# A long-convolution and expert-routing kernel: fifteen key differences for sixteen keys, the first transform in row halves, the last channel quarter in two halves, and a new order

## The chip, the cores and the metric

The kernel runs on one core of one Trainium2 chip. The core has five engines with queues of their own, each working strictly in its list's order: PE (TensorE, matrix products, with its weight loads shown as PEld), DVE (VectorE), ACT (ScalarE), POOL (GpSimd) and SP, which here issues transfers. [...] The metric is the device time of one execution in microseconds, the median of several runs.

## The reference

The input is 2048 positions by 512 channels, in single precision. Two layers follow one another, each with a residual.

The first normalizes each position, and convolves each channel along the 2048 positions with a kernel of its own, `K[d, l] = 2 Re sum_n C[d, n] exp(A[d, n] dt[d] l)` over 128 modes, plus a skip term. The reference uses FFTs of length 4096.

The second normalizes again and routes to experts:

```python
q = jnp.einsum("nd,dhc->nhc", xf, w_q)            # 32 heads, 2 x 128
s1 = jnp.einsum("nhd,ed->nhe", q[..., :dk], k1)   # 16 keys
s2 = jnp.einsum("nhd,ed->nhe", q[..., dk:], k2)   # 16 keys
i1, i2 = argmax of s1, argmax of s2               # K = 1
top_e = i1 * 16 + i2                              # one of 256 experts
act = gelu(einsum(xf, u[top_e]))
out = einsum(softmax of one score = 1, act, v[top_e])
```

So the scores serve only to find the largest of sixteen in each of 64 groups a position (32 heads, two halves); their size is not used.

## The kernel before, in words

**Constants ahead.** The product of `w_q` and the keys doesn't depend on the position. `w_piece(n)`, 32 pieces, loads a piece of `w_q` (tile wq), multiplies it with the keys (L822), turns it (L830), and stores groups of four pieces to DRAM (w_d, L837). Later the whole is loaded back as w_q, 512 by 1024, and split into a high and a low part (w_hi, w_lo, L917 and L918), so that a product of three fast terms replaces one of full precision.

**Convolution.** It is done by hand-made transforms, in four quarters c = 0 to 3 of 128 channels. For 32 table blocks of 16 channels, POOL builds phase tables (pg, L551) and magnitude tables (mg, L582 and L588), ACT takes sines and cosines (L638 to L641), DVE multiplies them (L645 to L658), and PE sums over the modes (kps, L684): this gives the convolution kernel. pg and mg have two buffers each, so POOL may not fill mg for block i before PE has used block i - 2. Input (u) and kernel (k) then go through the same two transforms. Stage 1 (`stage1`, L465, tiles s1u and s1k) takes eight groups a call in two half-jobs of four groups; ACT copies each from PSUM (L468). Stage 2 (L482, tiles s2yu and s2yk) takes 32 frequencies in eight jobs of four. DVE multiplies the spectra (L726 to L729); in the last quarter POOL does a part (L737), after a copy by ACT (L733). The first inverse transform (ia, L758) has eight jobs a quarter and needs all eight products; its copies (T, L766, in the last quarter L771) go to DRAM (t_d) for c = 0 to 2, and stay on chip for c = 3. All of this shares seven PSUM banks (psA).

**Hand-over and expert part.** When the tables are used up, their memory becomes that of w_q, w_hi and w_lo. Eight blocks b of 256 positions follow: second inverse transform (ib, L1029, from Tb, xt and cb loads), mean and variance, scores (sc, L1143: per 128 positions 4 x 3 x 2 matmuls of 512 columns), products with the experts' first matrix (xu, L1150), then on DVE the maximum of each group (mx, L1165), a comparison with it (eq, L1169), and a product with powers of two (kq, L1174), which POOL adds up within the group (ks, L1180) so that DVE reads the index from the exponent (L1187 to L1191). One-hot masks (oh, L1269), their counts on PE (cnt, L1279), and the product with the experts' second matrix (o, L1313 and L1316) end a block.

**Order.** Each step is entered in a plan with engine, cost, reads and writes, and gets a number. The tuple `ORDER` lists the numbers; the steps are issued in that order, so it fixes each engine's queue, SP's transfers too. The costs are planning numbers and change nothing in the program by themselves.

Of the kernel before, what the change touches and what calls it, by code (L numbers as in the profile page):

```python
# [27 lines left out]
def view(t, off, dims):  # L28
# [135 lines left out]
def kernel(ctx, tc, xa, xb, xt, lar, aim, cre, cim, ldt, dsk, wq, ka, kb, ue, ve,  # L164
# [10 lines left out]
    G.memset(halfpi, math.pi / 2)  # L175
    G.memset(epst, EPS)
    make_identity(nc, ident)

    t_d = dram.tile([P, 3, 2, 2048], F32, name="t_d")
    e_d = dram.tile([P, 11, 256], F32, name="e_d")  # L180
    w_d = dram.tile([P, 4, 1024], F32, name="w_d")

    I = {}

    ab = ctx.enter_context(ExitStack())
    wk = ab.enter_context(tc.tile_pool(name="wk", bufs=1, side="left"))
    ka_s = wk.tile([P, 32], F32, name="ka_s")
# [1248 lines left out]
```

## Time and profile before

| | |
|---|---|
| median of 3 runs | 515.38 us (513.67 to 515.58) |
| the profiled execution | 516.5 us, span 514.7 us |
| mean clock of TensorE in it | 0.977 of full |
| PE busy | 459.3 us, 89% |
| DVE busy | 411.3 us, 80% |
| POOL busy | 321.7 us, 63% |
| ACT busy | 300.4 us, 58% |
| transfers | 61.32 MB, 119 GB/s on average |

Busy time is a share of the whole span, and the kernel has stages with different limits, so each stage is read by itself. A row of the profile reads: line of the kernel, engine, operation, output tile and input tiles, partitions by elements; "x" gives the number of instructions. Matmuls overlap, so the mean duration of one is longer than its distance to the next. In the chain of waits, each piece is what the next one waited for; "issue" there is time for which the profile shows no releaser. A product in single precision issues two load and two matmul instructions.

### The profile page before, as it was taken

The numbers are of one execution on the slowest core, as the hardware profiler recorded it, in microseconds if no ns is written. First come the engines' busy times: TensorE is split into PE (matmuls) and PEld (weight loads), VectorE is DVE, ScalarE is ACT, GpSimd is POOL, SyncE is SP. The second block draws the span as 40 slices with busy tenths as digits, with TensorE's granted clock in tenths as the row PEclk, the third lists the DMA queues.
The fourth block names the chain that finished last, engine by engine and source line by source line (L and its number), as shares of the span: only waits on it lengthen the run. The fifth ranks groups of instructions, "written<-read, shape, count | busy, mean of one in ns | idle before, by whom it ended". The sixth has DMA issues, their size and how long they took to land.

```text
span 514.7 us, 16728 instructions
## 1 busy us (share of the span) xinstructions
PE 459.3 (89%) x7206; PEld 392.3 (76%) x7206; DVE 411.3 (80%) x724; ACT 300.4 (58%) x596; POOL 321.7 (63%) x342
## 2 busy tenths in 40 slices
PE   0275889999999999999998949999999999999995
PEld 0143669888998999899997947877878888786784
DVE  5999898899959988999727573888969596979983
ACT  4867799967897598858964442334152341426240
POOL 4989979999999999996807011760351506263330
PEclk9998699999999999999999998999999999999998
DMA  7969474224043102611056984400162141010012
GB/s 255 385 206 383 127 276 146 65 84 175 3 177 96 40 3 82 202 50 44 1 208 183 292 266 155 144 1 1 54 186 91 30 137 42 1 43 0 2 42 85
DMA packets 27362, 61.32 MB, mean 119 GB/s; under 512 B 2932, under 2 KB 14456, under 8 KB 26136
## 3 DMA queue, kind: packets, MB, share of 16 engines
q1 hardware_dynamic: 27136, 60.11, 34.8%
q8 instruction: 57, 0.93, 0.8%
q10 hardware_dynamic: 152, 0.13, 0.1%
q14 instruction: 17, 0.14, 0.1%
HBM read 46.21 MB, written 14.02 MB: 117 GB/s over the span
## 4 chain that ended last, share of the span: by engine, by line
PE 62%; DVE 15%; ACT 11%; DMA 5%; issue 4%; POOL 2%; SPq 0%; DVEq 0%; ACTq 0%; POOLq 0%
PE sc L1143 18%; PE ia L758 8%; PE s2yk L482 4%; PE kps L684 4%; PE s1k L465 3%; PE xu L1150 3%; PE s2yu L482 3%; PE o L1316 3%; PE cnt L1279 3%; PE s1u L465 2%; PE ib L1029 2%; DMA wq<-wq 2%; ACT t L641 2%; PE bc L1247 1%; ACT t L639 1%
## 5 line engine op out<-in xcount | busy, mean ns | idle before, releaser
L551 POOL TENSOR_TENSOR pg<-PS 128x1024 int32<-128x1024 int32 x32 | 68.9, 2152 | 0.5
L582 POOL TENSOR_TENSOR mg<-TS 128x1024 f32<-128x1024 f32 x32 | 62.6, 1958 | 7.8 <-PE kps L684 4.1
L1180 POOL TENSOR_TENSOR ks<-kq 128x512 f32<-128x512 bf16 x16 | 18.9, 1182 | 56.6 <-DVE kq L1174 53.4
L1269 DVE TENSOR_SCALAR oh<-idxb,ec_s 128x2048 bf16<-128x2048 bf16 (+1 forms) x72 | 46.3, 708 | 8.9 <-ACT idxb L1251 7.0
L758 PE MATMUL ia<-ca_s,U 128*128 128x128 f32 x256 | 49.6, 276 | 0.0
L1053 POOL TENSOR_TENSOR vs<-hc 128x256 f32<-128x256 f32 x8 | 6.5, 815 | 62.5 <-ACT hc L1076 62.5
L1143 PE MATMUL sc<-w_hi,hhi 128*128 128x512 f32 x128 | 45.1, 434 | 0.0
L639 ACT ACTIVATE t<-t,halfpi 128x512 f32<-128x512 f32 x64 | 42.4, 662 | 2.1
L1143 PE MATMUL sc<-w_lo,hhi 128*128 128x512 f32 x128 | 40.8, 400 | 0.0
L638 ACT ACTIVATE t<-pg 128x512 f32<-128x512 int32 x64 | 38.9, 608 | 3.0 <-DVE gf L646 2.0
L1143 PE MATMUL sc<-w_hi,hlo 128*128 128x512 f32 x128 | 40.6, 399 | 0.0
L641 ACT ACTIVATE t<-pg 128x512 f32<-128x512 int32 x64 | 38.2, 608 | 3.2 <-POOL pg L551 2.1
L758 PEld LDWEIGHTS ia<-ca_s,U 128*128 128x128 f32 x256 | 38.9, 192 | 0.0
L758 PE MATMUL ia<-ca_s,yk 128*128 128x128 f32 x192 | 38.2, 281 | 0.4 <-DVE mg L658 0.4
L588 POOL TENSOR_TENSOR mg<-TS 128x512 f32<-128x512 f32 x32 | 37.4, 1171 | 0.4
L684 PE MATMUL kps<-mg 128*32 128x64 f32 x1024 | 34.0, 231 | 3.3 <-DVE mg L658 1.6
L465 PE MATMUL s1u<-c_s,xs 128*64 128x128 f32 x512 | 33.4, 277 | 2.5 <-DVE xs L502 1.6
L482 PE MATMUL s2yk<-yk,c_s 128*128 128x128 f32 x256 | 35.0, 283 | 0.5 <-DVE U L729 0.4
L684 PE MATMUL kps<-gf 128*32 128x64 f32 x1024 | 33.5, 228 | 0.9 <-issue 0.9
L482 PEld LDWEIGHTS s2yk<-yk,c_s 128*128 128x128 f32 x256 | 30.8, 192 | 3.7 <-issue 1.4
L465 PE MATMUL s1k<-c_s,k 128*64 128x128 f32 x512 | 32.8, 284 | 0.3 <-ACT yk L468 0.3
L482 PE MATMUL s2yu<-yu,c_s 128*128 128x128 f32 x256 | 32.6, 279 | 0.3
(197 smaller groups left out, 1380.9 us busy)
## 6 DMA issues: line engine op xcount, KB each, us to landing
wq<-wq SPq DMA_DIRECT2D x25, 512.0 KB, 4.1
t_d<-T SPq DMA_DIRECT2D x24, 256.0 KB, 4.2
Tb<-t_d SPq DMA_DIRECT2D x8, 768.0 KB, 6.0
x<-xa SPq DMA_DIRECT2D x8, 512.0 KB, 6.0
xs<-xb SPq DMA_DIRECT2D x16, 256.0 KB, 4.8
xt<-xt SPq DMA_DIRECT2D x8, 512.0 KB, 3.9
out<-ob SPq DMA_DIRECT2D x7, 512.0 KB, 3.0
c_s<-wq SPq DMA_DIRECT2D x4, 512.0 KB, 8.4
```

The costliest lines, as they stand in the source:

```text
L465: T.matmul(ps[64 * k:64 * k + 64, g, :], lhs8(4 * n + g), c1_s[:, k], start=True, stop=True)
L482: T.matmul(ps[:, k, :], c2_s[:, kk, :], y[:, :, kk, :], start=True, stop=True)
L551: G.tensor_tensor(view(pg, 0, [[32, 2 * NC], [8, 4], [1, 8]]), view(t["PS"], 1024 + off, [[1, 2 * NC], [128, 4], [0, 8]]), view(t["PS"], 8 ...
L582: G.tensor_tensor(view(mg, 0, [[96, NC], [8, 8], [1, 8]]), view(ts, 512 + 8 * o, [[8, NC], [1, 8], [0, 8]]), view(ts, 8 * o, [[8, NC], [0, ...
L588: G.tensor_tensor(view(mg, 64, [[96, NC], [8, 4], [1, 8]]), view(ts, 1536 + o, [[1, NC], [64, 4], [0, 8]]), view(ts, 1024 + 8 * o, [[8, NC ...
L638: A.activation(p, pg[:, :, k], AF.Abs)
L639: A.activation(p, p, AF.Sin, scale=-SINSCALE, bias=halfpi)
L641: A.activation(p, pg[:, :, k], AF.Sin, scale=SINSCALE)
L684: T.matmul(kps[32 * q:32 * q + 32, 2 * g + h, :], m[:, d, 64:96], m[:, d, 0:64], start=(e == 0), stop=(e == 1))
L758: T.matmul(ps[:, g, :], t[:, 4 * n + g].rearrange("p a b -> p (a b)"), ca_s[:, s, :], start=(s == 0), stop=(s == 1))
L1143: T.matmul(ps[:, 512 * h:512 * h + 512], t[x_][:, q, ts], I[w_][:, q, 512 * h:512 * h + 512], start=(q == 0 and x_ == w_), stop=(q == 3 an ...
L1269: V.tensor_scalar(oh[:, :, 0:ln], t["idxb"][:, :, sl], S["ec"][:, 4 * e + j:4 * e + j + 1], None, op0=ALU.is_equal)
```

## The change

**Differences.** After the loads, fifteen keys of each half have the sixteenth subtracted (`differ`). The scores are then fifteen differences a group, 960 columns for 1024, 480 a PSUM bank. The largest is raised to zero by a small operation on DVE (128 by 64, 16 times); where no difference equals it, the sixteenth key is meant: no power is added, and the index formula is bounded to give it. POOL adds two overlapping halves of eight, with the power of the shared one halved. w_d, w_q, w_hi, w_lo, the key tiles and the copies `out2` get narrower accordingly (not shown).

**Stage 1.** Its constant mixed four interleaved channels over all 128 rows, with zeros between the rows of different channels. Now it has two channels a 64-row half; each matmul takes 64 rows and 64 columns, the halves write to two PSUM banks, and both banks are copied after both half-jobs.

**Last quarter.** `SEGS` = 2 for c = 3: stage 2 of the kernel takes half of the channels (16 of 32 groups, 64 columns) and eight frequencies a job, still eight jobs. The first four jobs need only the first two stage-1 calls, and the first four jobs of ia only the first four products.

**Order.** All numbers from 6 on move by one (`differ` is 6), and the list is another one. Read by its steps: before, the last six pieces of w_q's product stand on PE behind the last table block, among the stage-2 jobs of the last quarter; now all 32 stand ahead of the end of the third quarter's ia, with the last store of w_d ahead of that quarter's t_d stores. Before, all eight stage-1 half-jobs of the last quarter's kernel stand behind block 30; now six stand ahead of blocks 30 and 31, and two of the stage-2 jobs as well. At the start, twelve loads of wq stood ahead of the last block of x, now sixteen; eight first products of pieces stood ahead of the first block's kps, now eleven; the exponentials for the second half of the channels moved behind the arctangent on ACT. The planning costs of some steps are changed.

```diff
+        def differ():
+            for t, o in ((ka_s, 0), (kb_s, 16)):
+                V.tensor_scalar(t[:, o:o + 15], t[:, o:o + 15], t[:, o + 15:o + 16], None, op0=ALU.subtract)
...
     def stage1(dst, lhs8, kt, nm, r, tiles, key):
+        job, k = {}, None
         for n in range(2):
-            job = {}
             def mm(n=n, job=job):
-                ps = bank(job, f"{nm}_{n}")
-                for g in range(4):
+                if n == 0:
+                    for h in range(2):
+                        bank(job, f"{nm}_{h}", h)
+                for g in range(4 * n, 4 * n + 4):
                     for k in range(2):
-                        T.matmul(ps[64 * k:64 * k + 64, g, :], lhs8(4 * n + g), c1_s[:, k], start=True, stop=True)
-            def ev(n=n, job=job):
-                A.copy(dst()[:, 8 * kt + 4 * n:8 * kt + 4 * n + 4].rearrange("p g k d -> p g (k d)"), job["ps"])
-            k = plan.add("PE", 0.99, mm, r=r, t=tiles, take="psA", n_mm=16)
-            plan.add("ACT", 0.48, ev, w=[key + (kt, n)], t=tiles, give="psA", after=[k])
+                        for h in range(2):
+                            hs = slice(64 * h, 64 * h + 64)
+                            T.matmul(flat(job[h], 64)[64 * k:64 * k + 64, g], lhs8(g)[hs], c1_s[hs, k], start=True, stop=True)
+            k = plan.add("PE", 0.56, mm, r=r, t=tiles, take=() if n else ("psA", "psA"), after=[k] if n else [], n_mm=32)
+        for h in range(2):
+            def ev(h=h, job=job):
+                A.copy(dst()[:, 8 * kt:8 * kt + 8, :, 2 * h:2 * h + 2],
+                       flat(job[h], 64).rearrange("p g (k d) -> p g k d", d=2))
+            plan.add("ACT", 0.52, ev, w=[key + (kt, h)], t=tiles, give="psA", after=[k])
...
+            sg, nk = k4 * ns // 8, 4 * ns
+            g_, k_ = slice(32 * sg // ns, 32 * (sg + 1) // ns), slice(nk * (k4 % (8 // ns)), nk * (k4 % (8 // ns)) + nk)
+            kts = range(4 * sg // ns, 4 * (sg + 1) // ns)
+            deps = [("yk", c, kt, n) for kt in kts for n in range(2)]
+            def mm(job=job, g_=g_, k_=k_, k4=k4, nk=nk):
+                ps = flat(bank(job, f"s2yk{c}_{k4}"), 512 // nk)
+                for kk in range(k_.start, k_.stop):
+                    T.matmul(ps[:, kk - k_.start, :], c2_s[:, kk, :], spectrum(c, "yk")[:, g_, kk, :], start=True, stop=True)
...
-        deps = [("P", c, k4) for k4 in range(8)]
         for n in range(8):
+            job, sg = {}, n * SEGS[c] // 8
+            deps = [("P", c, k4) for k4 in range(8 * sg // SEGS[c], 8 * (sg + 1) // SEGS[c])]
...
-                    T.matmul(ps[:, 512 * h:512 * h + 512], t[x_][:, q, ts], I[w_][:, q, 512 * h:512 * h + 512],
+                    T.matmul(ps[:, 512 * h:512 * h + 480], t[x_][:, q, ts], I[w_][:, q, 480 * h:480 * h + 480],
...
+            eq, ps = d["eq"].rearrange("p (b g) e -> p b g e", b=2), groups()
+            V.tensor_scalar_max(d["mx"], d["mx"], 0.0)
+            V.tensor_tensor(eq, ps, d["mx"].rearrange("p (b g) -> p b g", b=2).unsqueeze(3).to_broadcast([P, 2, 32, 15]),
+                            op=ALU.is_equal)
...
-            G.tensor_tensor(kt_, d["kq"][:, :, 0:8], d["kq"][:, :, 8:16], op=ALU.add)
+            G.tensor_tensor(kt_, d["kq"][:, :, 0:8], d["kq"][:, :, 7:15], op=ALU.add)
...
-            V.tensor_scalar_add(ef.rearrange("p h a -> p (h a)"), ei, -134.0)
+            V.tensor_scalar(ef.rearrange("p h a -> p (h a)"), ei, -134.0, -7.0, op0=ALU.add, op1=ALU.max)
...
-    c1 = np.zeros((4, 32, 2, 32, 4))
+    c1 = np.zeros((4, 32, 2, 32, 2))
     for q in range(4):
-        c1[q, :, 0, :, q] = np.cos(a)
+        c1[q, :, 0, :, q % 2] = np.cos(a)
...
-    keys = np.tile(np.concatenate([2.0 ** (15 - e)] * 2)[None], (128, 1))
+    key = 2.0 ** (15 - e[:15])
+    key[7] /= 2
+    keys = np.tile(np.concatenate([key] * 2)[None], (128, 1))
```

More of the change, by code (lines that the diff above doesn't have):

```diff
@@ L180 @@
     e_d = dram.tile([P, 11, 256], F32, name="e_d")
-    w_d = dram.tile([P, 4, 1024], F32, name="w_d")
+    w_d = dram.tile([P, 4, 960], F32, name="w_d")
     I = {}
@@ L729, in prod, with part, rest @@
                     V.tensor_mul(uv[0:64], pv[64:128], uv[0:64])
-            def part(job=job, k4=k4):
-                job["ki"] = wk.tile([P, 128, 4], F32, tag="kt", name=f"ki{k4}", bufs=3)
-                A.copy(job["ki"][0:64], job["ps"].rearrange("p k m -> p m k")[64:128])
-            def rest(job=job, k4=k4):
-                uv = four(c, Q[c]["U"], k4).rearrange("p g d k -> p (g d) k")
+            def part(job=job, k4=k4, nk=nk):
+                job["ki"] = wk.tile([P, 512 // nk, nk], F32, tag="kt", name=f"ki{k4}", bufs=3)
+                A.copy(job["ki"][0:64], flat(job["ps"], 512 // nk).rearrange("p k m -> p m k")[64:128])
+            def rest(job=job, views=views):
+                pv, uv, kv = views()
                 G.tensor_tensor(uv[0:64], job["ki"][0:64], uv[0:64], op=ALU.mult)
+            k = plan.add("PE", 0.98 if ns == 1 else 1.15, mm, r=deps + u_k + ["c2"], t=tiles, take="psA", n_mm=8 * ns)
             if c < 3:
-                plan.add("DVE", 2.14, prod, r=[("U", c, k4)], w=[("P", c, k4)], t=tiles, give="psA", after=[k])
+                plan.add("DVE", 2.14, prod, r=u_k, w=[("P", c, k4)], t=tiles, give="psA", after=[k])
             else:
@@ L744, in k_s2 @@
                 a = plan.add("ACT", 0.52, part, w=[ki], t=[ki], after=[k])
-                v = plan.add("DVE", 1.43, prod, r=[("U", c, k4)], t=tiles, give="psA", after=[k, a])
+                v = plan.add("DVE", 1.43, prod, r=u_k, t=tiles, give="psA", after=[k, a])
                 plan.add("POOL", 1.5, rest, r=[ki], w=[("P", c, k4)], t=[ki, f"U{c}"], after=[v])
@@ L776, in k_ia @@
             else:
-                a = plan.add("ACT", 0.70, lambda turn=turn: turn(A.copy, 0), w=[("T", c, n, 0)], t=[f"T{c}"], after=[k])
-                plan.add("DVE", 0.70, lambda turn=turn: turn(V.tensor_copy, 1), w=[("T", c, n, 1)], t=[f"T{c}"], give="psA",
+                a = plan.add("ACT", 0.75, lambda turn=turn: turn(A.copy, 0), w=[("T", c, n, 0)], t=[f"T{c}"], after=[k])
+                plan.add("DVE", 0.75, lambda turn=turn: turn(V.tensor_copy, 1), w=[("T", c, n, 1)], t=[f"T{c}"], give="psA",
                          after=[k, a])
@@ L912, in load @@
         def load(q=q):
-            I[q] = I["pre"].tile([P, 4, 256], F32, tag="xt" if q > 1 else "wq", name=f"w_q{q}").rearrange("p a b -> p (a b)")
+            I[q] = I["pre"].tile([P, 4, 256], F32, tag="xt" if q > 1 else "wq", name=f"w_q{q}").rearrange("p a b -> p (a b)")[:, 0:960]
             nc.sync.dma_start(I[q], w_d[:, q])
         plan.add("SP", 1.7, load, r=["pre"] + [("w_d", h) for h in range(8)], t=[w_t], w=[("w_q", q)], lag=2.6)
-        plan.add("ACT", 0.95, lambda q=q: A.copy(I["hi"][:, q], I[q]), r=[("w_q", q)], w=[("w_hi", q)], t=[w_t])
-        plan.add("DVE", 1.15, lambda q=q: V.tensor_sub(I["lo"][:, q], I[q], I["hi"][:, q]), r=[("w_q", q), ("w_hi", q)],
+        plan.add("ACT", 0.90, lambda q=q: A.copy(I["hi"][:, q], I[q]), r=[("w_q", q)], w=[("w_hi", q)], t=[w_t])
+        plan.add("DVE", 1.08, lambda q=q: V.tensor_sub(I["lo"][:, q], I[q], I["hi"][:, q]), r=[("w_q", q), ("w_hi", q)],
                  w=[("w_lo", q)], t=[w_t], lock=True)
@@ L1155, in scores @@
         for q in range(4):
-            last = plan.add("PE", 1.48, lambda q=q: mm(q), t=tiles, after=[] if last is None else [last],
+            last = plan.add("PE", 1.40, lambda q=q: mm(q), t=tiles, after=[] if last is None else [last],
                             r=[(x, k) for x in tiles] + [("w_hi", q), ("w_lo", q)], take="psC" if q == 0 else None, n_mm=6)
@@ L1195, in gelu @@
             A.activation(act[:, k], jx["ps"], AF.Gelu_apprx_tanh, scale=t["rstd"][:, k:k + 1])
-        a = plan.add("DVE", 1.15, top, w=[m], t=[m], after=[last])
-        plan.add("DVE", 1.15, same, r=[m], w=[e], t=[m, e], give="psC", after=[a])
-        plan.add("DVE", 0.62, weigh, r=[e, "cst"], w=[kq_], t=[e, kq_], lock=True)
+        a = plan.add("DVE", 1.08, top, w=[m], t=[m], after=[last])
+        plan.add("DVE", 1.17, same, r=[m], w=[e], t=[m, e], give="psC", after=[a])
+        plan.add("DVE", 0.58, weigh, r=[e, "cst"], w=[kq_], t=[e, kq_], lock=True)
         plan.add("POOL", 2.8, gather, r=[kq_], w=[s_], t=[kq_, s_])
@@ L1299, in select @@
             if ln == 256:
-                plan.add("ACT", 0.52, high, r=[("wt", p)], w=[("whi", p)], t=[kA, kH])
+                plan.add("ACT", 0.64, high, r=[("wt", p)], w=[("whi", p)], t=[kA, kH])
                 plan.add("DVE", 0.62, low, r=[("wt", p), ("whi", p)], w=[("wlo", p)], t=[kA, kH, kL], lock=True)
```

60 lines of the change are left out of this document (32 added, 28 removed), and 162 rows, old and new, of the table ORDER.

## The prediction

> **What bounds the kernel now.** I read the page first (shares, slices), then busy time by stages, the waits of GpSimd, the chain of waits, and single instructions in order of time.
>
> ```profile
> span 514.7 us, 16728 instructions
> PE 459.3 (89%) x7206; PEld 392.3 (76%) x7206; DVE 411.3 (80%) x724; ACT 300.4 (58%) x596; POOL 321.7 (63%) x342
> PE   0275889999999999999998949999999999999995
> POOL 4989979999999999996807011760351506263330
> GB/s 255 385 206 383 127 276 146 65 84 175 3 177 96 40 3 82 202 50 44 1 208 183 292 266 155 144 1 1 54 186 91 30 137 42 1 43 0 2 42 85
> ```
>
> TensorE (PE) is full from slice 7 on, but for a hole near 300 us; GpSimd (POOL) is full from slice 2 to 18. Three stages, convolution, hand-over and expert part (columns: span, then busy us of PE, PEld, DVE, ACT, POOL):
>
> ```profile
> 57.00:256.00 199.00, 192.93 (x3621) 177.00 (x3611) 174.93 (x298) 165.39 (x315) 186.75 (x168) 0.99 0.29 97
> 256.00:310.20 54.20, 43.75 (x828) 39.85 (x826) 30.14 (x53) 26.68 (x57) 12.50 (x11) 0.97 0.71 228
> 310.20:514.70 204.50, 197.90 (x2286) 159.10 (x2286) 157.62 (x238) 69.55 (x116) 76.40 (x106) 0.98 0.20 63
> ```
>
> The convolution has two limits side by side: PE (192.9 of 199) and POOL (186.8). POOL's tables are a fixed amount of work, and they end here:
>
> ```profile
> 254.72 1.17 POOL L588 TENSOR_TENSOR mg<-TS 128x512 f32<-128x512 f32 x1
> ```
>
> at 255.9, with these waits before (us, times, longest):
>
> ```profile
> POOL mg L582 <- PE kps L684: 4.1, 2, 2.8
> POOL mg L582 <- DVE xs L502: 2.4, 1, 2.4
> POOL PS L542 <- DVE A L336: 1.9, 1, 1.9
> ```
>
> So whatever PE saves, the tables end at most 8.4 us earlier; 4.1 of it waits for PE. The hand-over, from the chain of waits:
>
> ```profile
> 257.55 3.64 PE s1k L465 x64
> ...
> 274.63 4.00 DMA wq<-wq
> ...
> 285.34 7.31 DMA w_q<-w_d
> ...
> 298.62 1.43 PE ib L1029 x85
> ...
> 304.77 4.99 issue
> 310.19 5.98 PE sc L1143 x18
> ```
>
> When the tables end, PE still owes all eight stage-1 half-jobs of the last quarter's kernel (x64 is four of them, 0.91 us each), then the last weight pieces go through DRAM in series (their load, their store, and w_q), and PE waits 5.0 us for the second block, where nothing but loads is open. From table end to first score: 310.2 - 255.9 = 54.3 us. The expert part is PE's (197.9 of 204.5).
>
> **The change, part by part.** *Stage 1.* A half-job was 8 products, 16 instructions of 128 columns, two column halves side by side; it becomes 32 instructions of 64 columns in four quadrants. The nearest row has 64 columns in four column tiles:
>
> ```profile
> 214.58 0.89 PE kps L684 x64
> ```
>
> 32 such take 0.45, with a start seam (126.71 to 127.74, 1.03 against 0.91, is 0.12) up to 0.57; I take 0.47, since the two half-jobs now mostly follow each other. No row shows two row halves at once: the other end is 0.91, or worse (rivals). At 64 half-jobs PE saves 64 x 0.44 = 28 us.
>
> [...]
>
> The copies out write runs of two floats; the copy with runs of four costs the same as the contiguous one, so I add nothing; double price would be 64 x 0.59 = 38 us on an ACT with 34 free, and it would bind.
>
> ```profile
> L468 ACT COPY yk<-s1k 128x512 f32<-128x512 f32 x32 | 18.0, 595 | 2.0 <-PE s1k L465 1.7
> L766 ACT COPY T<-ia 128x512 f32<-128x512 f32 x24 | 13.7, 590 | 3.7 <-PE ia L758 3.7
> ```
>
> One wait is new: a half-job pair takes two of the seven PSUM banks at its start, and ACT's copies follow only after the second half. Should PE, with its next list entries queued behind, stand still 0.47 us for it at each of 32 pairs, that is 15 us, more than the 13 that stay over below; I take 0, because ACT is free 34 us in this stage, and the other end goes into C.
>
> *Order.* In the new list six of the eight half-jobs and the last six weight pieces stand ahead of the tables' end. That is 6 x 0.91 = 5.5 us, and six pieces at twice 11.7 / 25 (this row is one of two like groups, 25 pieces each), 5.6:
>
> ```profile
> L822 PE MATMUL wps<-wq,ka_s 128*32 128x128 f32 x200 | 11.7, 309 | 19.3 <-DMA wq<-wq 17.0 <-issue 2.0 <-DVE mg L658 0.2
> ```
>
> With 4.1 us of earlier tables PE must find 15 us before the end and has 28, so POOL sets it: 255.9 - 4.1 = **251.8**. This holds until a half-job costs 0.91 - 15/64 = 0.68. The bounds are 247.5 (all three waits gone) and later than 255.9 (a rival).
>
> *Last quarter in two halves.* Stage 2 there has twice the matmuls, 64 columns instead of 128, and the full 128-column weights each time:
>
> ```profile
> 174.11 0.89 PE s2yk L482 x8
> ```
> ```profile
> L255 PEld LDWEIGHTS va<-dv,eq x4: 188/191/192, 63.5 to 63.8; 128*128 128x128 f32 x4
> L255 PE MATMUL va<-dv,eq x4: 275/276/324, 63.5 to 63.9; 128*128 128x64 f32 x4
> ```
>
> Four loads whose first and last starts are 0.3 us apart: 0.10 each (the view rounds to tenths) under 64-column matmuls, as under 128 columns (0.89 / 8 = 0.11). So the weights set the pace and a job goes from 0.89 to 16 x 0.11 = **1.76**; the other end is 0.89, half the columns at full gain. I take 1.76, its rows being the same shape. Products and transform:
>
> ```profile
> 268.36 0.69 DVE L726 TENSOR_TENSOR yu<-s2yk,U 128x512 f32<-128x512 f32 x1 [5.28 <-ACT ki L733]
> 269.09 0.68 DVE L727 TENSOR_TENSOR U<-s2yk,U 64x512 f32<-64x512 f32 x1
> ```
> ```profile
> 258.50 0.69 DVE L658 TENSOR_TENSOR mg<-mg,t 128x512 f32<-128x512 f32 x1 [0.63 <-ACT t L639]
> ```
> ```profile
> 280.36 0.39 PE L758 MATMUL ia<-ca_s,yu 128*128 128x128 f32 x2
> ```
> ```profile
> 294.49 0.28 PE L758 MATMUL ia<-ca_s,U 128*128 128x128 f32 x1
> ```
> ```profile
> 282.41 0.74 ACT L771 COPY T<-ia 64x256 f32<-64x256 f32 x2 [1.41 <-PE ia L758]
> 283.18 0.86 DVE L771 COPY T<-ia 64x256 f32<-64x256 f32 x2 [3.32 <-ACT T L771]
> ```
>
> Now the new hand-over, in us after the tables' end, along PE's new list: last table product on DVE 3.3 (259.2 - 255.9); last kernel generation 1.0, at 4.3; two stage-2 jobs and two half-jobs, 2 x 1.76 + 2 x 0.47, at 8.8; ACT's two copies 1.1 (0.59 each, overlapping), at 9.9; four stage-2 jobs, at 16.9. The first half's products (four at 1.45 from 3.3, then POOL's 1.3) are ready at 10.4, and the second's at 16.2 or soon after PE's last job, while the first four transforms run: hidden, and what is gained by the halves. Eight transforms, 14.2 (280.4 to 294.6), at 31.1; last copies 1.6, at 32.7; inverse and mean to the first score 298.6 to 310.2 without the 5.0 wait, 6.6, at **39.3**. Gain 54.3 - 39.3 = 15.0. The weights' way through DRAM (274.6 to 292.7) drops out, since their pieces are stored before and w_q can load once the last tables are used, some 30 us ahead of its use. With stage 2 at 0.89 the sum is 34.1, gain 20.2.
>
> *Fifteen differences.* 384 matmuls go from 512 to 480 columns.
>
> ```profile
> 329.40 1.40 PE sc L1143 x6
> ```
> ```profile
> 401.63 1.44 PE o L1316 x12
> ```
>
> Those are 233 ns for 512 columns and 120 ns for 256, so 0.443 ns a column: 32 x 0.443 x 384 = **5.4 us**. On DVE two large operations (and a smaller one) lose a sixteenth and one small one is added, 16 times each:
>
> ```profile
> L1165 DVE TENSOR_REDUCE mx<-sc 128x64 f32<-128x1024 f32 x16 | 19.5, 1220 | 5.7 <-PE sc L1143 5.6
> L1189 DVE TENSOR_SCALAR ef<-ei 128x64 f32<-128x64 int32 x16 | 6.6, 414 | 0.6
> ```
>
> The maximum and the comparison, of one size, give 2 x 19.5/16 = 2.4 back, the new one takes at most 6.6 (as the last row, of its size): net under +4.2 us on an engine busy 157.6 of 204.5, under PE's cover; 0, or +4.2 where that cover fails. POOL's key sums keep their size (76.4 of 204.5 busy), and the casts and copies of the narrower weights shrink in the hand-over's shadow: 0. The subtraction from the keys, once, on two small tiles, lies beside the first loads: 0 to 0.4.
>
> Sum: -4.1 - 15.0 - 5.4 = -24.5. The profiled execution took 516.5 (span 514.7 and 1.8 around it): 492.0. The median shown, 515.38, is 1.1 below that execution: **491**.
>
> **The rivals.** *A. Weights are loaded faster than their rows say* under the shorter stage 2: gain 29.7, **486**. For it: weight loads overlap in kps (64 in 0.89, from column tiles). Against: L255.
>
> *B. The start and the loads take part of it back.* Sixteen instead of twelve wq loads stand ahead of the last block of x, eleven instead of eight weight pieces ahead of the first kernel generation. 512 KB at 385 GB/s is 1.36 us, four make 5.4 on POOL, whose first reuse of a table waits for that generation (the large decay exponentials, moved behind the arctangent on ACT, push the same way); and if the loads of the second block are still the last to land, the 5.0 stay: -14.1, **501**. For it: slices 1 and 3 at 385 GB/s. Against: POOL has other tables to build meanwhile.
>
> *C. Row halves do not overlap*, or a floor under the starts or the banks hold them: a half-job stays near 0.91. PE's busy time of the first two stages, 236.7, plus 7.0 for the last quarter, plus 2.8 of idle behind the last transform, puts the first score between 303.5 and 309.6 (without and with the 6.1 idle before 256); 306.5 gives -3.7 - 5.4, **506**. For it: no row shows overlap.
>
> *D. Slower: the issue order breaks the column pairs too.* A channel group issues first column half with both row halves, then the second. If row halves exclude each other, only the middle two of four can pair: three turns of 2 x 0.056 instead of two of 0.111, 1.33 a half-job, +0.42 x 64 = 27 us where PE already binds: 506 + 27, **533**. It decides from 1.05 us a half-job (64 x 0.14 = 9.1 eats C's gain).
>
> **How the numbers follow.** Forecast 0.43, A 0.22, B 0.15, C 0.12, D 0.08. The range holds the first three: low end A with POOL's other 4.3 us of waits gone too, 481, and 2 us more for what new lists may save in the expert part's 6.6 idle us, 479; high end just behind B, 504. C and D, 0.20, are left out. A measurement here tells about 0.5% (2.6 us) from no change. Faster: forecast, A, B and two thirds of C, 0.88; same 0.04 (the rest of C); slower 0.08.
>
> **What would show it.** Right: stage-1 groups of 16 matmuls in some 0.23 us where they follow each other; POOL's last table at 250 to 254 without waits for kps; no wq or w_q transfer in the chain behind it; stage 2 of the last quarter near 1.76 a job; first score near 291; score groups of six at 1.32 us, the expert part near 199 us. Wrong: half-jobs above 0.68, which hand the end of the tables back to PE; stage-1 copies well above 0.6; a POOL gap before 60 us; DVE waits turning up ahead of scores.

## The result: 538.1 us, slower by 4.6%

The changed kernel took 538.09 us (median of four, 537.56 to 539.94); the kernel before took 515.18 beside it. The ratio is 1.046, with a 95% interval of 1.042 to 1.049. The forecast was 491. Medians here are over all runs of a kernel; ratios leave disturbed runs of both kernels out, so a ratio can differ a little from the quotient of two medians, and of the later runs the profiles of e10 (512.4 us), e14 (529.4, where its ratio rests on 521.0 and 522.6) and e15 (512.4) are of disturbed ones.

The page of the changed kernel, the span and two rows of busy time and granted clock:

```profile
span 536.2 us, 18906 instructions
PE 454.2 (85%) x8294; PEld 392.6 (73%) x8294; DVE 424.3 (79%) x742; ACT 306.9 (57%) x600; POOL 327.9 (61%) x342
PEclk9999868999998798999999599899999999999999
```

PE's busy time fell by only 5 us, and its clock reads below 9 in eight slices where it did in four. The same stages as in the prediction (columns: span, then busy us of PE, PEld, DVE, ACT and POOL, granted clock, DMA share, GB/s):

```profile
57.00:278.60 221.60, 193.39 (x4723) 173.71 (x4726) 179.54 (x307) 172.86 (x331) 191.43 (x170) 0.93 0.32 105
278.60:330.30 51.70, 47.19 (x852) 45.92 (x846) 30.84 (x54) 23.74 (x45) 10.13 (x9) 0.87 0.54 176
330.30:536.20 205.90, 191.07 (x2292) 158.71 (x2286) 168.26 (x255) 72.81 (x120) 84.78 (x109) 0.99 0.20 65
```

GpSimd's last table ends at 278.6 instead of 255.9, the hand-over takes 51.7 instead of 54.3, the expert part 205.9 instead of 204.5. So all of the loss stands ahead of the end of the tables, where PE is now idle for 28.2 us of the 221.6 behind 57 us (before: 6.1 of 199). The rows of single instructions that set these bounds:

```profile
42.16 0.44 PE L696 MATMUL kps<-mg 128*32 128x64 f32 x8
277.44 1.17 POOL L600 TENSOR_TENSOR mg<-TS 128x512 f32<-128x512 f32 x1
330.34 0.70 PE L1169 MATMUL sc<-w_hi,hhi 128*128 128x480 f32 x2
```

The first kernel generation comes at 42.2 (before: 36.9). The groups of stage 1 (busy us, mean ns | idle just before), first of before, then of after:

```profile
L465 PE MATMUL s1u<-c_s,xs 128*64 128x128 f32 x512 | 33.4, 277 | 2.5 <-DVE xs L502 1.6 <-ACT yu L468 0.9
L465 PE MATMUL s1k<-c_s,k 128*64 128x128 f32 x512 | 32.8, 284 | 0.3 <-ACT yk L468 0.3
```
```profile
L475 PE MATMUL s1u<-c_s,xs 64*64 64x64 f32 x1024 | 24.1, 234 | 7.9 <-issue 3.2 <-DVE xs L514 1.5 <-DVE mg L666 1.5
L475 PE MATMUL s1k<-c_s,k 64*64 64x64 f32 x1024 | 22.2, 236 | 5.3 <-issue 3.7 <-ACT yu L480 0.8 <-DVE gf L661 0.6
L480 ACT COPY yu<-s1u 128x512 f32<-128x512 f32 x32 | 19.0, 642 | 14.9 <-PE s1u L475 14.9
```

The row halves do overlap: 66.2 us of stage 1 became 46.3. But 2.8 us of waits before it became 13.2, half of it called issue, which is time in which PE waited for nothing that the profile shows. Two such waits, as they stand in time, and the waits of the whole run that matter here (us, times, longest):

```profile
162.35 3.03 PE L475 MATMUL s1k<-c_s,k 64*64 64x64 f32 x105 [2.29 <-issue]
177.65 0.59 PE L475 MATMUL s1u<-c_s,xs 64*64 64x64 f32 x11 [3.21 <-issue]
```
```profile
POOL mg L594 <- PE kps L696: 20.6, 9, 6.9
PE s1k L475 <- issue: 3.7, 3, 2.3
PE s1u L475 <- issue: 3.2, 1, 3.2
```

GpSimd now waits 20.6 us for kernel generations on PE (before: 4.1). Its own work up to the end of the tables is the same 233 us in both kernels, so what it waits is what the end of the tables inherits.

### The profile page after: what moved, and what is told of

It is laid out like the page before. It is cut to its first block, busy times and chain, and to the rows that moved or that the text cites. A ratio compares the mean times of both kernels' runs of the same rounds, so it can differ in the third digit from the quotient of the medians.

```text
span 536.2 us, 18906 instructions
## 1 busy us (share of the span) xinstructions
PE 454.2 (85%) x8294; PEld 392.6 (73%) x8294; DVE 424.3 (79%) x742; ACT 306.9 (57%) x600; POOL 327.9 (61%) x342
## 5 line engine op out<-in xcount | busy, mean ns | idle before, releaser
L594 POOL TENSOR_TENSOR mg<-TS 128x1024 f32<-128x1024 f32 x32 | 62.6, 1957 | 27.0 <-PE kps L696 20.6
L737 PE MATMUL s2yk<-yk,c_s 128*128 128x128 f32 (+1 forms) x320 | 46.9, 304 | 2.7 <-ACT yk L480 1.4
L1301 DVE TENSOR_SCALAR oh<-idxb,ec_s 128x2048 bf16<-128x2048 bf16 (+1 forms) x72 | 48.7, 737 | 0.0
L737 PEld LDWEIGHTS s2yk<-yk,c_s 128*128 128x128 f32 x320 | 43.1, 215 | 4.7 <-ACT yk L480 1.7
L1169 PE MATMUL sc<-w_hi,hhi 128*128 128x480 f32 x128 | 42.4, 413 | 0.0
L783 PEld LDWEIGHTS ia<-ca_s,U 128*128 128x128 f32 x256 | 41.0, 202 | 1.1 <-DVE U L753 1.1
L1169 PE MATMUL sc<-w_hi,hlo 128*128 128x480 f32 x128 | 38.9, 385 | 0.0
L1169 PE MATMUL sc<-w_lo,hhi 128*128 128x480 f32 x128 | 38.8, 384 | 0.0
L847 PE MATMUL wps<-wq,ka_s 128*32 128x128 f32 x200 | 12.2, 321 | 25.8 <-DMA pb<-wq 16.9
L696 PEld LDWEIGHTS kps<-mg 128*32 128x32 f32 x1024 | 26.0, 118 | 9.7 <-issue 5.4
L783 PEld LDWEIGHTS ia<-ca_s,yk 128*128 128x128 f32 x192 | 30.1, 197 | 3.7 <-ACT t L650 1.4
```

The source lines that it names most:

```text
L594: G.tensor_tensor(view(mg, 0, [[96, NC], [8, 8], [1, 8]]), view(ts, 512 + 8 * o, [[8, NC], [1, 8], [0, 8]]), view(ts, 8 * o, [[8, NC], [0, ...
L696: T.matmul(kps[32 * q:32 * q + 32, 2 * g + h, :], m[:, d, 64:96], m[:, d, 0:64], start=(e == 0), stop=(e == 1))
L737: T.matmul(ps[:, kk - k_.start, :], c2_s[:, kk, :], spectrum(c, "yk")[:, g_, kk, :], start=True, stop=True)
L783: T.matmul(ps[:, g, :], t[:, 4 * n + g].rearrange("p a b -> p (a b)"), ca_s[:, s, :], start=(s == 0), stop=(s == 1))
L1169: T.matmul(ps[:, 512 * h:512 * h + 480], t[x_][:, q, ts], I[w_][:, q, 480 * h:480 * h + 480], start=(q == 0 and x_ == w_), stop=(q == 3 an ...
L1301: V.tensor_scalar(oh[:, :, 0:ln], t["idxb"][:, :, sl], S["ec"][:, 4 * e + j:4 * e + j + 1], None, op0=ALU.is_equal)
```

## The experiments

Three theories at first: O, the new order is the cost; H, the row halves and the falling clock; I, PE waits for its instructions.

**1. The parts alone.** All three code changes with the old order; the differences alone; the row halves alone; the new order with stage 1 whole.

```diff
 e1  ORDER of before (numbers shifted), code of after
 e2  before, +differ() behind the key load, 960 instead of 1024 score columns, ORDER of before
 e3  before, +stage1() of after, ORDER of before
 e4  after, stage1() of before, ORDER of after
 e1, e3: a pair's first copy moves behind its second half
```

> All three code changes (row halves in stage 1, last quarter in two halves, fifteen differences) with the issue order of the kernel before; a stage-1 copy that came too early for both halves is moved behind the second half, nothing else moves. The changed kernel took 538.1 us, the one before 515.2. Theory O (the new order is what costs the time: first kernel generation at 42 instead of 37 us, weight loads ahead of it, last table end at 278.6 instead of 255.9): with the old order the code's savings show and the old waits remain, 500 to 510, last table end near 255. Theory H (the row halves themselves cost it: while they run the granted clock falls, 0.93 instead of 0.99 between 57 us and the last table end): 525 to 540, granted clock below 0.95 between 60 and 255 us. Theory I (PE waits for its own instructions, 16.6 thousand instead of 14.4 thousand): 515 to 530 with the clock near 0.99 and idle time called issue before the stage-1 lines of over 10 us.

> The fifteen differences alone, on the kernel before with its order; the one subtraction from the keys is put behind their load. All theories of the slowdown leave this part out of the convolution, so 509 to 513: score groups of six at 1.31 us instead of 1.40 take 5 to 6 us off PE in the expert part. If the longer chain on VectorE (maximum, the clamp, comparison) binds instead, the expert part stays at 204 to 206 us and the time at 514 to 517.

> The row halves of stage 1 alone, on the kernel before with its order (the copies of a pair behind its second half). Theory O: PE saves up to 20 us of stage 1, the last table end stays at 255 or comes up to 4 us earlier, 505 to 513. Theory H: granted clock below 0.95 between 60 and 255 us, last table end at 262 or later, 522 to 535. Theory I: clock near 0.99 there, last table end at 255 to 262, idle time called issue before stage 1 of over 10 us, 515 to 522.

> The changed kernel with its own new order, but stage 1 in whole columns as before (512 fewer matmuls; last quarter's halves and the differences stay). Theory O: PE has 20 us more of stage 1 to do in the same order, so 538 or slower, up to 555. Theory H: the clock is back at 0.98 or more between 60 us and the last table end, which comes at 250 to 262; 500 to 515. Theory I: 515 to 530.

Measured: e1 535.7 us (ratio 1.049, 1.038 to 1.060), e2 512.4 (1.001, 0.996 to 1.006), e3 538.7 (1.055, 1.046 to 1.064), e4 522.4 (1.022, 1.013 to 1.031). With the old order the row halves alone cost as much as the whole change, so O falls as the main cause; but e4 shows that the new order, together with the last quarter's halves, costs something too, 10 us against e2. e4 lies in I's range alone; e1 and e3 lie where H had them or above. Neither H nor I is settled by these four. In e2 the expert part shrank as forecast (below), but the first kernel generation came at 40.2 instead of 36.9 and the last table at 258.2 instead of 255.9; at the start VectorE stood waiting for the keys:

```profile
10.00 0.23 DVE L289 TENSOR_SCALAR ka_s<-ka_s 128x15 f32<-128x15 f32 x1 [2.69 <-DMA ka_s<-ka]
40.19 0.44 PE L697 MATMUL kps<-mg 128*32 128x64 f32 x8 [0.98 <-POOL TS L588]
```

In e3 PE's waits before stage 1 have a pattern that no data explains (us, times, longest):

```profile
PE s1u L474 <- DVE gf L657: 4.9, 4, 2.0
PE s1k L474 <- DVE mg L669: 2.9, 3, 1.5
PE s1k L474 <- DVE mg L665: 2.9, 2, 1.7
```

Stage 1 reads nothing of `gf` or `mg`. What these table products free is the PSUM bank of the sine or cosine that they read: `trig` takes its bank from the same seven as stage 1. So theory B was added: the two banks that a pair holds.

**2. Banks.** Whole columns in the row halves' bank structure; fewer users of banks; shorter holding.

```diff
 e5  e3, but  T.matmul(job[h][64*k:64*k+64, x], lhs8(g), c1_s[:, k])   # 128 rows, 128 columns, two banks per pair
 e6  e3, nine entries of ORDER moved, and in trig(), cos only:
-        p = flat(bank(...), 32)
+        p = pg[:, :, k].bitcast(F32)      # in place over the phases, no bank
 e7  e3, first half of each pair moved right ahead of its second in ORDER
 e8  before, with the edit of e6
```

> The kernel before with stage 1 in whole columns, but in the bank structure of the row halves: a pair of half-jobs writes two of the seven PSUM banks from its first half on, and both copies come after its second half; issue order of the row-halves run (538.7 us). The temporaries of the sines and cosines take banks of the same seven. Theory B (the banks are the cost: the pair holds two of them for longer, so PE and ScalarE wait for a free one): as slow as the row halves or slower, since PE has 20 us more to do, 535 to 560. Theory W (the row halves' own instructions are the cost: twice the count, small, a falling clock): 513 to 520.

> The row halves alone (538.7 us, old order), but the 64 cosines are written in place over the phases in SBUF and take no bank; the sines still take one each. Theory B: waits for banks shrink from 25 us on PE to a few, last table end near 255 or earlier, 500 to 520. Theory W: 530 to 540.

> The row halves alone, old order, but the first half of each pair is moved right ahead of its second half, so that the two banks are held for about 1.1 us of PE and two copies. Theory B: a pair holds its two banks for some 5 bank-us instead of 10; waits for banks on PE fall to under 10 us, 508 to 525. Theory W: 530 to 540.

> Control: the kernel before with the cosines in place over the phases and nothing else changed. Theory B: before, PE waits 1.7 us and ScalarE 2.7 us for banks, so little is to be had: 511 to 516. If reading the cosines from SBUF is dearer for VectorE: its table products are then longer than 0.69 us and the time is up to 525.

Measured: e5 531.2 us (1.034, 1.024 to 1.044), e6 567.8 (1.107, 1.098 to 1.117), e7 534.7 (1.039, 1.029 to 1.049), e8 560.1 (1.091, 1.083 to 1.099). e5 runs the very matmuls of before and loses 17 us, between the ranges of B and W: under the old order the bank structure alone is a cost. e7 contradicts B's price: held for shorter, the banks give back 4 us, not 14 to 31. e6 and e8 settle nothing about banks, since the control (e8) was hit by something else: with its second operand in SBUF a table product took 1.2 to 1.5 us on average instead of 0.68, and GpSimd's tables, running beside it, went from 1.17 to 1.44 us (mean ns after the comma):

```profile
L661 DVE TENSOR_TENSOR mg<-mg,pg 128x512 f32<-128x512 f32 x32 | 48.6, 1518 | 0.0
L594 POOL TENSOR_TENSOR mg<-TS 128x512 f32<-128x512 f32 x32 | 46.0, 1440 | 0.4
```

**3. Clock or count.** Each stage-1 product twice, so that PE is not idle. Beside it, three steps towards a better kernel: the subtraction later, the weight pieces early, and the last quarter in halves.

```diff
 e9   e3, and
+                            for _ in range(2):
                                 T.matmul(flat(job[h], 64)[...], lhs8(g)[hs], c1_s[hs, k], start=True, stop=True)
 e10  e2, differ() some 4 us later on VectorE
 e11  e10, weight pieces 20 to 31 where the new ORDER has them
 e12  e11, SEGS = (1, 1, 1, 2)
```

> The row halves alone with the old order (538.7 us, granted clock 0.93 between 57 and 279 us) with every stage-1 product issued twice into the same place: the result is the same, PE has about 25 us more to do, and a half-job costs about what whole columns cost. Known beside it: whole columns in the same bank structure take 531.2 with the clock at 1.00. Theory C (what the row halves lose beyond the banks, 7.5 us, comes from PE standing idle so much that its clock is lowered): with more work the clock stays above 0.97 there and the time is 527 to 538, no longer than with half the work. Theory N (the number of small instructions is the cost): 550 to 565, with idle time called issue ahead of stage 1. Theory P (PE's work sets the pace in this form): 545 to 560 without it.

> The fifteen differences alone with the order of before (512.4 us, of which the expert part 198.6 against 204.6, but the first kernel generation at 40.2 instead of 36.9 us, since VectorE stood 2.7 us before the subtraction for the load of the keys). Now the subtraction stands behind the cosine and sign preparation of the second part, some 4 us later on VectorE, when the keys have landed. If that wait is what took back half of the gain: first kernel generation at 36.9 to 37.6, last table end at 255 to 257, 506 to 510. If the start isn't handed on to the tables' end: 510 to 513.

> As the run with the late subtraction (fifteen differences, old order), but the weight pieces of the last three groups stand where the new order has them, ahead of the last tables; stage 1 whole, last quarter in one half. The hand-over from last table end to first score was 54.2 us before and 46.5 in the run with the new order and whole stage 1. If the weights' way through DRAM was what the hand-over waited for: 44 to 50 us from last table end to first score; PE has 5 to 6 us more before the last table end, which moves by 0 to 6: 500 to 509. If it was not: hand-over stays at 52 to 54 and the time is 507 to 514.

> As the run with the early weights, and the last quarter's stage 2 and transform in two halves as in the change. Its rows price a stage-2 job at 1.9 us instead of 0.9, so PE has 8 us more between the last table and the first score, and up to 7 us of products under the first four transforms to gain: the same as the run before it to 8 us slower, 503 to 515. A gain of over 2 us would show that the products were what the transforms waited for.

Measured: e9 584.7 us (1.137, 1.127 to 1.147), e10 511.5 (0.994, 0.988 to 0.999), e11 519.5 (1.014, 1.008 to 1.020), e12 517.5 (1.010, 1.005 to 1.016). e9 lies above all three ranges. C had it no longer with more work, and it is 46 us longer; N's sign is there, and stronger than N had it. e11 and e12 lie above what was expected of them as well, and the intervals of the two overlap, so the halves of the last quarter show no clear gain. PE's waits in e9's convolution, and the DMA traffic from 180 to 200 us in 40 slices of 0.5 us (GB/s):

```profile
PE s1k L475 <- issue: 12.7, 8, 3.4
PE kps L696 <- issue: 11.3, 7, 3.7
PE s1u L475 <- issue: 5.2, 6, 1.5
```
```profile
GB/s 467 385 434 393 115 49 49 16 33 0 0 0 0 0 0 0 33 0 0 0 0 0 0 33 0 0 0 0 0 0 33 0 16 0 0 0 0 0 0 147
```

Between slice 9 and the last, all that moves but for one slice of 16 are single slices of 33 GB/s, that is 16 KB, seven slices or 3.5 us apart. They are packets of the instruction queue, of which e9 has 81 where e3 has 65 and before 57:

```profile
q8 instruction: 57, 0.93, 0.8%
```
```profile
q8 instruction: 81, 1.33, 0.9%
```

Sixteen packets more for 4096 instructions more (2048 matmuls and as many weight loads) make 256 instructions, or 128 matmuls, a packet. The trace's records of this queue beside the long issue waits of PE (us):

```
kernel   16 KB packet: start, took     PE's wait: until (length)
before   307.4, 1.00                   309.77 (4.99)
after    159.9, 0.93                   162.35 (2.29)
after    175.4, 0.92                   177.65 (3.21)
after    227.5, 1.58                   230.50 (1.08)
e10      308.5, 1.01                   310.96 (4.51)
e11      315.7, 0.96                   317.93 (3.44)
```

Each wait ends 1.3 to 1.6 us after a packet has come. And each begins at the same place in the stream: counted in the trace, PE has by then started 193 instructions more than a multiple of 256. That holds for all six rows, for all seven issue waits of the changed kernel behind 50 us that are 0.3 us or longer, and for all 26 such waits of e9; waits for other engines begin anywhere. PE was waiting for instructions.

A row-half half-job is 32 matmuls with their weight loads, a quarter of a packet: at e9's one packet in 3.5 us it can be fed in an estimated 0.87 us, though it runs in 0.58 (half of the 1.16 that 64 take). Whole columns need half of that, 0.44, and run in 0.91.

This does not explain e3. Between 57 us and its last table PE has no issue wait of 0.3 us or more, but its granted clock is lower than e5's, which has the same banks and order (first e3, then e5, up to the last table):

```profile
57.00:279.00 222.00, 185.17 (x4496) 169.10 (x4497) 175.35 (x296) 167.49 (x314) 186.85 (x168) 0.92 0.25 86
```
```profile
57.00:272.50 215.50, 193.02 (x3617) 175.05 (x3610) 175.73 (x298) 165.99 (x315) 186.92 (x168) 1.00 0.26 89
```

So under the old order the 7.5 us by which e3 is slower than e5 come without starvation. e9 doesn't settle whether they are the clock's, since PE starves there (its clock in the convolution is 0.96); that stays open.

In e11 GpSimd's last table came at 265.6 instead of 256.7, and the hand-over shrank by 2.0 only. The last table in e10 and in e11:

```profile
255.55 1.17 POOL L601 TENSOR_TENSOR mg<-TS 128x512 f32<-128x512 f32 x1
```
```profile
264.47 1.17 POOL L601 TENSOR_TENSOR mg<-TS 128x512 f32<-128x512 f32 x1
```

The 8.9 us are not simply PE's extra work. With the weight pieces moved, a load of x goes out behind a store of weights, at 201.2 us (165.3 in e10); VectorE stands 6.06 us for it, and GpSimd later waits 7.13 us for a product of VectorE that comes 7.9 us later than in e10:

```profile
206.03 0.69 DVE L512 TENSOR_TENSOR xs<-xs,pc 128x512 f32<-128x512 f32 x1 [6.06 <-DMA xs<-xb]
244.24 1.95 POOL L595 TENSOR_TENSOR mg<-TS 128x1024 f32<-128x1024 f32 x1 [7.13 <-DVE gf L659]
```

GpSimd's waits for kernel generations are what they were (4.0 us, 4.1 in e10). The changed kernel has no such wait for x there, so e11 prices early weight pieces only in its own list.

**4. What divides the 16 us between e4 and the changed kernel.** Under the new order: banks alone, then instructions alone. And the wait of 4.5 us before the second block's end.

```diff
 e13  after, stage1() as in e5
 e14  after, and in stage1()
-                for g in range(4 * n, 4 * n + 4):
+                for g in range(4 * n, 4 * n + 4, 2):
-                            T.matmul(flat(job[h], 64)[64*k:64*k+64, g], lhs8(g)[hs], c1_s[hs, k], ...)
+                            T.matmul(flat(job[h], 64)[64*k:64*k+64, g:g+2], lhs8(g)[hs],
+                                     c1_s[hs, k].unsqueeze(1).to_broadcast([64, 2, 64]), ...)
 e15  e10, last PE and VectorE entries of inv1 moved behind the first four of sc0 in ORDER
```

> The changed kernel with its own order, stage 1 in whole columns but in the row halves' bank structure (two banks from the first half of a pair on, both copies after the second). It stands between the run with the new order and whole stage 1 in single banks (522.4 us) and the changed kernel (538.1). Theory B (banks are the larger part): 532 to 545. Theory S (the row halves' twofold count of PE instructions is the larger part: PE waits for its next 16 KB of instructions, which come no closer than 3.4 us apart in the run with doubled products): 522 to 530, with hardly an idle time called issue on PE before the last table end.

> The changed kernel with half as many stage-1 instructions of twice the width: each row-half product is issued for every second channel group only and streams its 64 columns twice, into its own place and its neighbour's. The products of every second group are left out of the result; banks, copies, order and PE's streaming time of a half-job stay as in the change (538.1 us). Theory S: no idle time called issue ahead of stage 1, the last table end 8 us or more ahead of 278.6, 518 to 530. Theory B: 534 to 540.

> The run with the fifteen differences and the late subtraction (511.5 us), with the last quarter of the second block's inverse transform moved on PE behind the first four groups of scores. PE stands 4.5 us at 306.5 there, six products ahead of the end of that block. Theory S (it waits for instructions: a refill of 16 KB starts 2 us later and the wait ends 1.4 us after it): the scores behind it are few long instructions, but the next refill is due at the same place of the stream, so a wait of 2 to 4.5 us comes before or after the first scores: 506 to 511. The theory of the prediction (a load of the second block is late): the first score starts near 307 without a wait, 505 to 508.

Measured: e13 523.1 us (1.020, 1.013 to 1.026), e14 526.0 (1.017, 1.007 to 1.026), e15 510.0 (0.986, 0.982 to 0.990). Stages of e13 and then of e14, as above:

```profile
57.00:271.00 214.00, 200.66 (x3789) 182.43 (x3791) 179.03 (x307) 172.04 (x333) 192.29 (x171) 0.98 0.32 107
271.00:317.60 46.60, 44.02 (x769) 42.30 (x765) 30.90 (x54) 23.55 (x45) 10.14 (x9) 1.00 0.58 196
317.60:522.10 204.50, 190.57 (x2290) 158.49 (x2286) 168.30 (x255) 72.86 (x120) 84.67 (x109) 0.99 0.19 65
```
```profile
57.00:267.90 210.90, 187.29 (x3806) 164.54 (x3810) 179.08 (x307) 171.72 (x329) 191.85 (x170) 0.95 0.31 108
267.90:320.20 52.30, 47.16 (x752) 45.32 (x747) 30.78 (x54) 23.81 (x45) 10.12 (x8) 0.87 0.54 179
```

and what is left of issue waits on PE in e14's convolution:

```profile
PE kps L703 <- issue: 0.6, 1, 0.6
```

With the new order the bank structure costs nothing (e13 against e4: 523.1 and 522.4). Halving the count at the same streaming time (a half-job by itself takes 0.67 us in e14, 0.69 in the changed kernel) brings the last table from 278.6 to 267.9, and the issue waits before stage 1 are gone. GpSimd's waits for kernel generations shrink by the same 10.7 us, from 20.6 to 9.9, and are 11.1 in e13:

```profile
L601 POOL TENSOR_TENSOR mg<-TS 128x1024 f32<-128x1024 f32 x32 | 62.6, 1955 | 16.2 <-PE kps L703 9.9
```
```profile
L599 POOL TENSOR_TENSOR mg<-TS 128x1024 f32<-128x1024 f32 x32 | 62.5, 1955 | 18.2 <-PE kps L701 11.1
```

So that part comes from the count of instructions. The clock goes with it: around the waits until 162.35 and 177.65 the changed kernel has a granted clock of 0.83, and GpSimd then stands for PE:

```profile
160.00:190.00 30.00, 23.72 (x557) 21.10 (x554) 18.94 (x32) 19.16 (x39) 22.16 (x21) 0.83 0.39 120
182.12 1.95 POOL L594 TENSOR_TENSOR mg<-TS 128x1024 f32<-128x1024 f32 x1 [6.44 <-PE kps L696]
```

From 57 us to the last table the clock is 0.98 in e13 and 0.95 in e14, against 0.93. How the 10.7 us divide between standing still, a lower clock and the halved number of weight loads was not tried.

The hand-over stays at 52.3 in e14's profile and is 46.6 in e13's. There another thing decides, the clock. Stage 2 of the last quarter, four jobs, in the changed kernel and in e13, each with the 5 us that hold most of it:

```profile
293.46 11.97 PE L737 MATMUL s2yk<-yk,c_s 128*128 128x64 f32 x64 [1.21 <-ACT yk L480]
298.60:303.60 5.00, 5.00 (x26) 5.00 (x25) 2.22 (x4) 2.06 (x3) 1.37 (x2) 0.50 0.32 106
```
```profile
287.64 7.36 PE L742 MATMUL s2yk<-yk,c_s 128*128 128x64 f32 x64 [0.74 <-ACT yk L485]
291.00:296.00 5.00, 5.00 (x46) 5.00 (x46) 3.77 (x7) 2.97 (x5) 3.79 (x3) 1.00 0.67 220
```

The same 64 matmuls take 4.6 us more, in large part at a granted clock of 0.50, after a stretch in which PE had stood still for 1.2 us out of five; in e13 it stood for 0.7 and kept its clock. What lowered the clock was not tried.

In e15 the first score comes at 303.9 instead of 311.3 in e10, and the wait has split, as S had it:

```profile
303.92 0.70 PE L1170 MATMUL sc<-w_hi,hhi 128*128 128x480 f32 x2
309.41 0.26 PE L1056 MATMUL ib<-cb,Tb 128*32 128x64 f32 x3 [1.05 <-issue]
319.95 0.25 PE L1056 MATMUL ib<-cb,Tb 128*32 128x64 f32 x2 [2.79 <-issue]
```

4.51 us became 3.84, the sum of the two. e10's wait begins when PE has started 9921 instructions; e15's begin at the same 9921 and at 10177, one packet on. So the wait hangs on the place in the stream, whatever work stands there. e15 is the fastest kernel of the study by the medians: 1.4% below the kernel before by the ratio, 5.2% below the changed one. That it gains on e10 is not shown: their intervals overlap, and both profiled executions have a span of 510.6 us.

The stages of all, from the profiles (us):

| kernel | last table ends | hand-over | expert part | span |
|---|---|---|---|---|
| before | 255.9 | 54.3 | 204.5 | 514.7 |
| e1, code of after, old order | 283.7 | 53.3 | 197.4 | 534.4 |
| e10, differences | 256.7 | 54.6 | 199.3 | 510.6 |
| e11, and early weights | 265.6 | 52.6 | 198.4 | 516.6 |
| e12, and last quarter in halves | 267.9 | 51.3 | 198.4 | 517.6 |
| e4, new order, stage 1 whole | 270.5 | 46.5 | 204.8 | 521.8 |
| e13, the same in two banks | 271.0 | 46.6 | 204.5 | 522.1 |
| e14, halves, half the count | 267.9 | 52.3 | 207.4 | 527.6 |
| after | 278.6 | 51.7 | 205.9 | 536.2 |

## Why the prediction was wrong

**Stage 1, "I take 0.47".** The mechanism was right: the 64 matmuls of a pair take 1.16 us at a granted clock of 1.00 (row below), 0.58 a half-job, and PE's busy time in stage 1 fell by 20 us instead of 28. C and D are out as far as they have the halves not overlap. What was missing is that a half-job has to be fed as well as run: over the whole run one kept PE busy for 0.72 us (46.3 / 64), and with the idle time before it for 0.93, above the 0.68 that the prediction gave as a sign of being wrong.

```profile
280.27 1.16 PE L475 MATMUL s1k<-c_s,k 64*64 64x64 f32 x64 [0.64 <-DVE gf L661]
```

**Banks, "I take 0".** Under the new order that holds to 0.7 us (e13 against e4). Under the old one it was 17 us (e5).

**"PE must find 15 us before the end and has 28, so POOL sets it: 251.8."** This step failed. The tables ended at 278.6: what PE saves did not reach GpSimd, which waited 20.6 us for kernel generations where the forecast had the 4.1 of before gone. Of the 26.8 us, halving the count of stage-1 instructions takes 10.7 away (e14) and whole columns in the same banks 7.6 (e13, 271.0): PE waits for its next packet (2.29 us until 162.35, 3.21 until 177.65), its clock falls beside that (0.83 from 160 to 190 us), kernel generations come late, and GpSimd waits for them (6.44 us until 182.12).

The other 16.1 (e14) or 19.2 (e13) do not hang on the count: they stay with half of it and with whole columns. e13 and e14 share with the changed kernel the order, the differences and the last quarter's halves. By themselves the differences move the end by 0.8 (e10 against before) and the halves by 2.3 (e12 against e11), so most of the rest is put to the order, by argument. GpSimd waits 5.8 (e14) and 7.0 us (e13) longer for kernel generations than before, and about as long again for results of VectorE. Which of the order's moves does it was not tried: early weight pieces alone move the end by 8.9 in e11, but through a late load of x. The first kernel generation at 42.2 instead of 36.9 is rival B's start; with the subtraction alone, placed late, it comes at 38.8 (e10).

**"A job goes from 0.89 to 1.76."** Right at a granted clock of 1.00: 7.36 / 4 = 1.84 in e13. In the changed kernel, at 0.70 from 293.6 us and 0.50 from 298.6, it was 2.99. The forecast had no term for the clock; it costs these jobs 4.6 us, most of the 5.1 by which the hand-over is longer than e13's (51.7 against 46.6).

**Hand-over 39.3.** It took 51.7. Beside the clock, PE came to the tables' end behind its list: half-jobs and two stage-2 jobs that the forecast had ahead of the tables' end stood between it and the last kernel generation, which ended 8.5 us after the tables instead of 4.3 (the two stage-2 jobs, and the last row of the generation). The clock and this make 9 of the 12.4 us that the sum is short; the rest lies in small pieces.

```profile
281.43 3.79 PE L737 MATMUL s2yk<-yk,c_s 128*128 128x64 f32 x32
...
286.85 0.29 PE L696 MATMUL kps<-gf 128*32 128x64 f32 x8
```

And "the weights' way through DRAM drops out" was worth 2.0 us (e11), not the most of 15: that chain ran beside PE's own work. The 5.0 us before the second block's end, put down to loads, were instructions (packet at 307.4, wait until 309.77; e15).

**Scores, -5.4.** Right, and lost again in the same stage. With the old order of the expert part it takes 197.4 to 199.3 us (e1, e2, e10, e11, e12) against 204.5; with the new order of that part 204.8, 204.5 and 205.9 (e4, e13, after). Between e1 and the changed kernel only the order differs: 197.4 and 205.9. The forecast costed the code of this stage and left its order out.

Rival B had the right sign and place for the start, and too small a price for the whole. No rival had the row halves' count: the prediction noted twice as many instructions and gave only their streaming time a price.

## What to carry to other kernels

Count the instructions of a change beside its busy time. Where a busy engine executes very short ones, a profile's "issue" waits and its instruction queue show whether they were fed. Here PE's busy time in stage 1 fell by 20 us and the waits before it rose from 2.8 to 13.2 us; with half the number of matmuls the tables ended 10.7 us earlier (e14). And price an order found anew stage by stage like any other edit: here it took back the gain of the scores, and most likely put off the end of the tables by more than the row halves did.

## What the runs showed of the hardware

- PE's instructions came in 16 KB packets of 256 (e9 has 16 packets more than e3 for 4096 instructions more). In e9 single packets came 3.5 us apart (180 to 200 us), and in the changed kernel no two came closer than 3.3 us. In the table a starved PE resumed 1.3 to 1.6 us after a packet had landed, and it stood each time 193 instructions behind a multiple of 256.
- With 64 rows and 64 columns, addressed to four quadrants, 64 matmuls took 1.16 us, 18 ns apart on average, though one takes 0.23 to 0.24 us (after, 280.27). The whole columns of two pairs, 64 matmuls too, took 3.64 us (before, 257.55).
- From 298.6 to 303.6 and from 303.6 to 308.6 PE was busy for all of 5.00 us with weight loads and 64 columns behind each, and its granted clock was 0.50 both times, after 0.70 in the 5 us before; from 308.6 to 313.6 it was 0.93. In e13 the same jobs ran at 1.00.
- A VectorE product of 128 by 512 with both operands in SBUF took 1.2 to 1.5 us on average with GpSimd working beside it (e8, three lines), where it took 0.68 with one in PSUM; GpSimd's tables went from 1.17 to 1.44 us (e8, 46 us slower by the medians).
